# Attention feeding a routed two-layer network: two batches share six rounds of sums and gate products

## The chip, the cores and the metric

The kernel runs on one core of one Trainium2 chip. The metric is the device time of one execution in microseconds (us). TensorE (PE) multiplies matrices into PSUM, ScalarE (ACT) and VectorE (DVE) read PSUM and work elementwise, GpSimd (POOL) works on SBUF alone, and SyncE (SP) issues most transfers.

## What is computed

Attention over q, k and v of shape (8 batches, 12 heads, 448 positions, 64), then a routed network over the 3584 tokens that it gives:

```
scores = cap * tanh(q k^T / sqrt(64) / cap)
attn   = exp(scores - max) / (sum of them + 1e-9)
x      = (attn v), heads side by side        # 3584 x 768
logits = x @ w_gate                          # 8 experts
assign each token to one expert, best logits first, 448 tokens an expert
out[tokens of e] = relu(x[tokens of e] @ w1[e]) @ w2[e]
```

## The kernel before, in words

`attention` (L18) works through 24 groups of four heads, three groups to a batch: group g belongs to batch b = g//3 and is the batch's m = g%3, so m=0, 1 or 2. The order of the instructions on PE, ACT, DVE and SP is the order in which the loop at L330 writes them; no scheduler moves them. A batch is called odd or even by b.

In one pass of the loop, group g's scores are made and group g-1's values are summed:

- `qk(g,r)`, r=0 to 6: four matmuls of 64x64 tiles that run beside each other write a score tile to PSUM (`psS`, **two** buffers). I call this a score step, and number the steps of a group 1 to 7. ScalarE's tanh (L201) reads the tile and so frees its buffer. After steps 2 and 4 ScalarE does the exp of the two tiles (L206, 128x1792), after step 7 that of three (128x2688). From g=18 on (`G2`, and in the first groups) the first two exps are put off until after one more tanh.
- `avq(g-1,..)`: seven value steps of the same size into two PSUM tiles `psA` (two buffers, both in use); `av_out` on DVE copies them to `xT` at the end of the pass and so frees them for the next pass.
- On DVE: `av_out` of the pass before, `tr` (32x32 transposes of the next group's k, later of its q, into `tk` and `tq`), `esum` (the additions that form the row sums: 'e2' and 'r' for group g-1, 'e1' for group g).

Beside this each batch has work of its own, done while the next batch's groups run:

- **Rounds** (`rnd`, L262): a PSUM tile `psM` (pool `pM`, two buffers) has four strips of 32 rows. Sums of exps (`ones` against `es`) and products with `w_gate` (`gw` against `xT`) are accumulated in it. A round is up to four matmuls of 128x32 tiles, one per strip, that run beside each other. Four rounds make a batch:

```
R=[gate(0)+sums(0),gate(1)+sums(1),sums(2),gate(2)]
```

  Rounds 0 and 1 use all strips, the sums those at the ends (0 and 3) and the gates the middle ones (1 and 2). In rounds 2 and 3 only strips 0 and 3 have work. `pos` says which place each pair of heads has in the strips.
- `logit_in` and `logit`: DVE copies the tile, PE transposes it, DVE takes reciprocals of the sums, multiplies and adds up to logits `L1`.
- `xt(b,p)`, p=0 to 5, for batches 0 to 3: PE transposes `xT`, DVE multiplies with the reciprocals into `xn`, and SP writes `xn` to DRAM after p=5. The other batches' turn comes after the attention.
- `on_logits` (18 small DVE instructions that prepare a batch's routing keys, from L519 on) and `on_turn` (one transposed block of keys).

Where they stand before: in m=0 the turns of p=0 to 3 of batch b-2 and `on_logits(b-2)`; in m=1 the turns of p=4 and 5, and rounds 0 and 1 of batch b-1; in m=2 rounds 2 and 3, and the logits of b-1. For b=6 and 7 the rounds are one stage earlier and spread over all three groups. The routing search (`Routing`) and the experts (`ffn_all`) follow the attention.

Of the kernel before, what the change touches and what calls it, by code (L numbers as in the profile page):

```python
# [17 lines left out]
def attention(nc, tc, c1, xp, ep, nv, pM, q, k, v, cap, w_gate, xs, L1, ident, on_logits, on_turn, NDEF, xd, setup, mark):  # L18
# [3 lines left out]
    B,H,S,D=q.shape  # L22
    CP=112; NJ=S//CP; NP=H//2; NQ=NP//2; E=w_gate.shape[1]; HG=2
    N=B*NQ
    pos=lambda p: (1+p//2+2*(p%2)) if p<4 else 5*(p-4)
    whole=lambda g: 0<g<N-1
    xT={}; rin={}; xn={}; spilled={}; todo=list(range(B-NDEF,B-2))
    def xt(b,p,late=None):
        if late and todo:
            for n in todo:  # L30
                xT[n]=late[1].tile([128,NP,S],F32,name="xTr",bufs=len(todo))
                nc.sync.dma_start(xT[n],spilled[n])
            todo.clear()
        if p==0:
            alt=late and (b in spilled and (b-B)%2 or b==B-1)
            xn[b]=(late[1] if alt else xp).tile([CP,NJ,H,D],F32,name="xn",bufs=1)
        ps=late[0].tile([128,512],F32,name="psL") if late else pM.tile([128,512],F32,name="psM")
        for j in range(NJ):
            nc.tensor.transpose(ps[:CP,j*128:(j+1)*128],xT[b][:,p,j*CP:(j+1)*CP],ident)  # L39
        def rest():  # L40
            if b==B-1 and p==NP-1:
                for j in range(NJ):
                    for h in range(2):
                        q=4*(p//2)+p%2+2*h; o=2*pos(p)+h
                        nc.scalar.activation(xn[b][:,j,q,:],ps[:CP,j*128+h*D:j*128+h*D+D],AF.Copy,scale=rin[b][:,j,o:o+1])
# [8 lines left out]
            (nc.gpsimd if late else nc.vector).tensor_tensor(xn[b][:,:,h0:h0+3:2,:],src,  # L54
                rin[b][:,:,2*pos(p):2*pos(p)+2].unsqueeze(3).broadcast_to([CP,NJ,2,D]),op=ALU.mult)
            if p==NP-1 or (late and p==3) or (b==B-1 and p==1):
                c0=0 if not late or p==1 or (p==3 and b<B-1) else 4*D if p==3 else 8*D; c1=2*(p+1)*D
                nc.sync.dma_start(xs[b*S:(b+1)*S,c0:c1].rearrange("(j p) d -> p j d",j=NJ),xn[b].rearrange("p j h d -> p j (h d)")[:,:,c0:c1])
        if late: return rest
        rest()  # L60
    with ExitStack() as ctx:
# [212 lines left out]
        def spill(bb):
            if B-NDEF<=bb<B-2:
# [2 lines left out]
        def logit_in(b):  # L278
            lgs[b]=xp.tile([128,S],F32,name="lg",bufs=1)
            nc.vector.tensor_copy(lgs[b],misc.pop(b)[:,:S])  # L280
        def logit(b,part=None,some=False,pool=None):
# [5 lines left out]
            if b not in rin: rin[b]=xp.tile([CP,NJ,H],F32,name="rin",bufs=max(NDEF,2))  # L287
            r=rin[b]
            if part is not None:
                va=ps[:CP,:].rearrange("p (a k) -> p a k",k=32)  # L290
                r2=xp.tile([CP,NJ*4],F32,name="rg1",bufs=1)
                nc.vector.reciprocal(r2,va[:,:,0])
                t=part
                nc.vector.tensor_tensor(t[:,:,0:4,:],va[:,:,16:24].rearrange("p (j g) e -> p j g e",g=4),
                    r2.rearrange("p (j g) -> p j g",g=4).unsqueeze(3).broadcast_to([CP,NJ,4,E]),op=ALU.mult)
            else:
                a,c=(1,5) if some else (0,6); n=2*(c-a)
                v3=ps[:CP,:].rearrange("p (j k) -> p j k",k=128)
                sm=ps[:CP,:].rearrange("p (j s k) -> p j s k",s=8,k=16)[:,:,0::7,a:c]
                rr=r.rearrange("p j (a h) -> p j h a",h=2)[:,:,:,a:c]  # L300
                nc.vector.reciprocal(rr,sm)
                t=xp.tile([CP,NJ,n,E],F32,name=f"lt{n}",bufs=1)
                nc.vector.tensor_tensor(t,v3[:,:,16+16*a:16+16*c].rearrange("p j (s e) -> p j s e",e=E),
                    r[:,:,2*a:2*c].unsqueeze(3).broadcast_to([CP,NJ,n,E]),op=ALU.mult)
            if not some:
                nc.vector.tensor_reduce(L1[:,b*NJ:(b+1)*NJ,:],t.rearrange("p j s e -> p j e s"),axis=AX.X,op=ALU.add)
                if b>=B-2: on_logits(b)
                if b==B-1: on_turn(b)
                if part is not None: nc.vector.tensor_copy(r.rearrange("p j (a k) -> p j a k",k=2)[:,:,0::5,:],r2.rearrange("p (j a k) -> p j a k",j=NJ,k=2))  # L309
                return  # L310
            t1=xp.tile([CP,NJ,5,E],F32,name="lt1",bufs=1)
            nc.vector.tensor_reduce(t1[:,:,4,:],t.rearrange("p j s e -> p j e s"),axis=AX.X,op=ALU.add)
# [16 lines left out]
        part=None  # L329
        for g in range(N):  # L330
# [7 lines left out]
            if g==N-5: vgate()  # L338
            if g==N-3: vback()
            qk(g,0); qk(g,1)  # L340
            early=bb-1<B-NDEF; late=not early
            if early and bb>0 and m<2:
                for p in ((0,1),(4,5))[m]: xt(bb-1,p)
            if m==2 and bb>=0:
                if early:
                    for r in (2,3): rnd(bb,r)
# [4 lines left out]
            if m==2 and bb>=0 and early:  # L351
                logit_in(bb); spill(bb)
            for w in ('e2','r'): esum(g-1,w)
            if g==N-6: vturn()
            if not head: qk(g,2)
            if order: avq(g-1,2,0)
            if m==2 and late: rnd(bb,3)
            qk(g,3)
            if order: qk(g,4)
            if m==0:  # L360
                if early and bb>0: xt(bb-1,2); xt(bb-1,3)
                if not early: rnd(bb,0); rnd(bb,1)
                if bb>0: on_logits(bb-1)
            if m==1 and bb>=0:
                if early: rnd(bb,0); rnd(bb,1)
                else:
                    rnd(bb,2); spill(bb)
                if bb>0: on_turn(bb-1)
            if m==2 and late: logit_in(bb)
            if m==2 and bb>=0 and (early or b==B-1): logit(bb)  # L370
            tr(g+1,1)
            if order: qk(g,5)
            else: qk(g,4)
            avq(g-1,0,1)
            if head: qk(g,6)
            avq(g-1,1,1)
            if not order: qk(g,5); avq(g-1,2,1)
            if not head: qk(g,6)
            if order: avq(g-1,2,1)
            avq(g-1,3,1)  # L380
            if not last: esum(g,'e1')
            if g: av_out(g-1,0); av_out(g-1,1)
            if m==2 and late and b<B-1: logit(bb)
        g=N-1; b=B-1
        rnd(b,0,1); rnd(b,1,1)
        logit_in(b)
# [795 lines left out]
```

## Time and profile before

| | us |
|---|---|
| runs | 861.40, 861.65, 862.03; median 861.65 |
| profiled execution, its own time | 861.69 |
| its span, first to last instruction | 859.9 |
| busy in the span: PE, ACT, DVE, POOL | 835.1, 582.3, 617.8, 390.5 |

The attention takes about the first 325 us of the span; the granted TensorE clock is 1.0 in all slices. From then on routing and experts follow, which the change does not touch. A chain row of the profile gives start, length, and what ran, merged where the same line repeats; a score or value step shows as 8 matmul records (x8), a full round as 8, a transposition as 1.

### The profile page before, as it was taken

The numbers are of one execution on the slowest core, as the hardware profiler recorded it, in microseconds if no ns is written. First come the engines' busy times: TensorE is split into PE (matmuls) and PEld (weight loads), VectorE is DVE, ScalarE is ACT, GpSimd is POOL, SyncE is SP. The second block draws the span as 40 slices with busy tenths as digits, with TensorE's granted clock in tenths as the row PEclk, the third lists the DMA queues.
The fourth block names the chain that finished last, engine by engine and source line by source line (L and its number), as shares of the span: only waits on it lengthen the run. The fifth ranks groups of instructions, "written<-read, shape, count | busy, mean of one in ns | idle before, by whom it ended". The sixth has DMA issues, their size and how long they took to land.

```text
span 859.9 us, 16866 instructions
## 1 busy us (share of the span) xinstructions
PE 835.1 (97%) x5838; PEld 589.2 (69%) x5838; DVE 617.8 (72%) x1992; ACT 582.3 (68%) x776; POOL 390.5 (45%) x556
## 2 busy tenths in 40 slices
PE   6999999999999998899999999999999999999997
PEld 3334444444433334588888888888898889999997
DVE  5787988989897967876877987968878864263210
ACT  6998898989899887575284584575655754544421
POOL 8210000000000007675377497595677668859851
PEclk9999999999999999999999999999999999999999
DMA  8979877585986007870863896986978959959921
GB/s 145 163 122 166 180 130 151 108 173 93 218 189 125 2 2 253 253 239 0 281 204 107 238 278 208 284 250 226 262 213 238 298 161 239 309 191 295 287 74 56
DMA packets 368485, 159.28 MB, mean 185 GB/s; under 512 B 287088, under 2 KB 355312, under 8 KB 367888
## 3 DMA queue, kind: packets, MB, share of 16 engines
q1 hardware_dynamic: 357728, 128.30, 60.9%
q0 software_dynamic: 4688, 22.02, 7.6%
q10 hardware_dynamic: 5984, 7.88, 2.6%
q8 instruction: 46, 0.75, 0.4%
q14 instruction: 39, 0.32, 0.1%
HBM read 107.24 MB, written 42.66 MB: 174 GB/s over the span
## 4 chain that ended last, share of the span: by engine, by line
PE 72%; issue 7%; ACT 7%; DVE 5%; DMA 3%; SPq 3%; POOL 2%; ACTq 0%; POOLq 0%; DVEq 0%
PE psH L995 22%; PE psH L1057 18%; PE psA L240 12%; PE psS L200 12%; ACT e L201 3%; PE psM L272 3%; ACT e L206 2%; DVE cmpD L587 1%; PE psM L39 1%; POOL out_dram L1015 1%; DMA xz<-xgl 1%; DMA xg<-xz 1%; SPq L1039 1%; SPq L861 1%; SPq L939 1%
## 5 line engine op out<-in xcount | busy, mean ns | idle before, releaser
L1057 PE MATMUL psH<-hh,w2h 128*128 128x448 f32 x672 | 185.3, 367 | 0.0
L201 ACT ACTIVATE e<-psS 128x896 f32<-128x896 f32 x168 | 147.5, 910 | 26.4 <-PE psS L200 20.8
L200 PE MATMUL psS<-tq,tk 64*64 64x448 f32 x1248 | 141.1, 542 | 8.3 <-ACT e L201 7.7
L206 ACT ACTIVATE e<-e,bias 128x1792 f32<-128x1792 f32 (+2 forms) x74 | 147.3, 1992 | 1.8
L995 PE MATMUL psH<-xgh,w1h 128*128 128x448 f32 (+1 forms) x384 | 141.8, 369 | 0.1
L995 PE MATMUL psH<-xgh,w1l 128*128 128x448 f32 (+1 forms) x384 | 140.0, 365 | 0.0
L995 PE MATMUL psH<-xgl,w1h 128*128 128x448 f32 (+1 forms) x384 | 135.4, 366 | 0.0
L873 POOL TENSOR_TENSOR w2l<-w2r,w2h 128x768 fp32r<-128x768 f32 x64 | 131.1, 2052 | 9.2 <-ACT w2h L866 8.4
L873 POOL TENSOR_TENSOR w1l<-w1r,w1h 128x768 fp32r<-128x768 f32 x62 | 114.9, 1854 | 43.2 <-ACT w1h L866 43.2
L240 PE MATMUL psA<-e,nv 64*64 64x448 f32 x1232 | 134.1, 538 | 0.0
L1057 PEld LDWEIGHTS psH<-hh,w2h 128*128 128x128 f32 x672 | 124.8, 188 | 7.7
L535 POOL TENSOR_SCALAR r_Bt<-r_b 112x4 f16<-112x4 int32 x1 | 0.2, 199 | 272.4 <-DVE rin L309 272.4
L1057 PE MATMUL psH<-hh,w2l 128*128 128x448 f32 x336 | 115.2, 366 | 0.0
L200 PEld LDWEIGHTS psS<-tq,tk 64*64 64x64 f32 x1248 | 46.9, 132 | 79.2 <-issue 45.8
L240 PEld LDWEIGHTS psA<-e,nv 64*64 64x64 f32 x1232 | 49.4, 133 | 66.0 <-issue 61.9
L995 PEld LDWEIGHTS psH<-xgh,w1h 128*128 128x128 f32 x384 | 72.5, 189 | 4.8 <-ACT xgh L956 0.3
L995 PEld LDWEIGHTS psH<-xgl,w1h 128*128 128x128 f32 x384 | 72.3, 188 | 4.4 <-DVE xgl L957 0.2
L866 ACT ACTIVATE w2h<-w2r 128x768 fp32r<-128x768 f32 x64 | 75.0, 1184 | 0.5 <-DMA w2r<-in_moe_w_dram 0.5
L995 PEld LDWEIGHTS psH<-xgh,w1l 128*128 128x128 f32 x384 | 72.2, 188 | 4.4
L1004 ACT ACTIVATE hh<-psH 128x448 fp32r<-128x448 f32 x56 | 30.4, 543 | 60.4 <-PE psH L995 57.0
L1057 PEld LDWEIGHTS psH<-hh,w2l 128*128 128x128 f32 x336 | 63.2, 188 | 4.0
L898 POOL DMA_INDIRECT xg<-xs,idx x32 | 32.5, 1014 | 65.3 <-DVE zz L750 37.6
(397 smaller groups left out, 1392.8 us busy)
## 6 DMA issues: line engine op xcount, KB each, us to landing
w1r<-in_moe_w_dram SPq DMA_DIRECT2D x64, 384.0 KB, 7.1
w2r<-in_moe_w_dram SPq DMA_DIRECT2D x64, 384.0 KB, 6.4
k<-in_k_dram SPq DMA_DIRECT2D x92, 112.0 KB, 3.0
q<-in_q_dram SPq DMA_DIRECT2D x92, 112.0 KB, 3.0
nv<-in_v_dram SPq DMA_DIRECT2D x88, 112.0 KB, 3.3
yb<-yq SPq DMA_DIRECT2D x56, 168.0 KB, 5.1
on<-yb SPq DMA_DIRECT2D x7, 1152.0 KB, 7.6
xs<-xn SPq DMA_DIRECT2D x4, 1344.0 KB, 6.3
```

Of the source, the lines that this page charges most:

```text
L39: nc.tensor.transpose(ps[:CP,j*128:(j+1)*128],xT[b][:,p,j*CP:(j+1)*CP],ident)
L200: nc.tensor.matmul(ps[w:w+64,h,:S],tks[g,0][hp,o,r*64:r*64+64],tks[g,1][hp,o,:],start=True,stop=True)
L201: nc.scalar.activation(ev(g,r),ps[:,:,:S],AF.Tanh,scale=sr[0])
L206: act=lambda: nc.scalar.activation(e,e,AF.Exp,scale=sr[1],bias=bias)
L240: for h in range(2): nc.tensor.matmul(avp[g,o][h*64:h*64+64,:S],z[w,r,h,:],ev(g,r)[w,h,:],start=r==0,stop=r==6)
L272: nc.tensor.matmul(ps[k*32:k*32+32,:S],lhs,rhs,start=r==0 and i==0,stop=r==last or (r==1 and k in (1,2)))
L866: nc.scalar.activation(view(h),r,AF.Copy)
L873: (eng or nc.gpsimd).tensor_tensor(view(l),r,view(h).bitcast(F32),op=ALU.subtract)
L898: g=nc.gpsimd.indirect_dma_start(out=row(j,n),out_offset=None,in_=xs,in_offset=bass.IndirectOffsetOnAxis(ap=res[p][0][:n,j:j+1],axis=0))
L995: nc.tensor.matmul(ps[:,o:C],a[:,c,:],b[:,c,o:],start=(m==0 and o==0),stop=(m==DC*3-1)); m+=1
L1004: nc.scalar.activation(h,ps[:,:C],AF.Relu)
L1057: nc.tensor.matmul(ps[:,:C],spl[p,2,hf,f//2][w][:,f%2,cc*128:cc*128+128],h[:,a,f],start=(m==0),stop=(m==nm-1))
```

## The change

Batches 0 to 5 are taken in pairs (0,1), (2,3), (4,5). For the odd batch of a pair the strips are mirrored (`pos(p,1)`, `oneb`): its sums stand in the middle strips and its gates at the ends. So the half-empty rounds of the even batch are filled with sums of the odd one: four rounds in `both`, two in `rest`, six for two batches where there were eight. Batches 6 and 7 keep `rnd`. Around it, everything is placed anew:

- in m=2 of an odd batch b: `both(b-1)` between score steps 4 and 5; no rounds in m=1 of an odd batch nor in m=2 of an even one;
- in m=1 of an even batch: `rest(b-1)` ahead of the value steps;
- logits of both batches of a pair: in m=0 and m=2 of the next even batch, split in two on DVE;
- turns: for an odd b as before, but on DVE those of p=2,3 behind the q transposes; for an even b the turns of p=0 to 3 go through two **score buffers** (`pairs`, one buffer for two turns), those of p=4,5 behind step 4 of m=1;
- `on_logits` in m=1 and m=2 of odd batches; `on_turn(3)` and `on_logits(4)` in b=6.

```diff
+    other=lambda b: b<B-2 and b%2==1
+    pos=lambda p,b=0: (0,4,1,5,2,3)[p] if other(b) else pos0(p)
...
+        def both(a):
+            b=a+1
+            for m in range(2):
+                for o in range(2): put(a,1+o,'g',m,o,m==0,m==1)
+                for h in range(2): put(a,3*h,'s',m,h,m==0,False)
+            for h in range(2):
+                put(a,3*h,'s',2,h,False,False); put(b,1+h,'s',0,h,True,False)
+            for h in range(2):
+                put(a,3*h,'g',2,h,False,True); put(b,1+h,'s',1,h,False,False)
+        def rest(b):
+            for o in range(2):
+                put(b,3*o,'g',1,o,True,False); put(b,1+o,'g',2,o,False,False)
+            for o in range(2):
+                put(b,3*o,'g',0,o,False,True); put(b,1+o,'s',2,o,False,True)
...
+            if new:
+                if not odd and m==0: turn.append(lambda: logit(b-2,lazy=True))
+                if not odd and m==2 and b<B-2: turn.append(lambda: logit(b-1,lazy=True))
...
+            two=xn_ and not odd and m==0
+            def pairs(p):
+                ps=pS.tile([128,2,512],F32,name="psS")
+                for i in range(2): xt(b-2,p+i,ps=ps[:,i])
+            if new and not odd and m==1: rest(b-1)
...
+            esum(g-1,'e2')
+            if two: pairs(0)
+            esum(g-1,'r')
...
+            if new and odd and m==2: both(b-1)
             tr(g+1,1)
+            if new:
+                if odd and m==0 and b>1: xt(b-2,2); xt(b-2,3)
+                if not odd and m==1 and xn_: xt(b-2,4); xt(b-2,5)
+                if odd and m==2: logit_in(b-1); spill(b-1)
+                if b==B-2 and m==1: spill(b-1); on_turn(3); on_logits(4)
+                if odd and m==1 and b>1: on_logits(b-3)
+                if odd and m==2 and b>1: on_logits(b-2)
+            if two:
+                qk(g,4); avq(g-1,1,1); pairs(2); qk(g,5); avq(g-1,2,1); qk(g,6)
```

In the logits of an odd batch the multiplication is three instructions of 112x128 in place of one of 112x384. POOL makes `oneb` with 13 more memsets in the first microseconds.

How PE's order moves in m=0 of an even batch (here b=2; psS is a score buffer, psA the value tiles). Before:

```order
L200 MATMUL psS<-tq,tk 64x448 x8
L39 MATMUL psM<-ident,xT 112x128 x8
L240 MATMUL psA<-e_942,nv 64x448 x8
L240 MATMUL psA<-e_982,nv 64x448 x4
L200 MATMUL psS<-tq,tk 64x448 x8
L39 MATMUL psM<-ident,xT 112x128 x8
L200 MATMUL psS<-tq,tk 64x448 x4
L240 MATMUL psA<-e_982,nv 64x448 x4
```

And in the change:

```order
L314 MATMUL psM<-ident,lg 112x128 x4
L247 MATMUL psA<-e_945,nv 64x448 x8
L247 MATMUL psA<-e_979,nv 64x448 x4
L41 MATMUL psS<-ident,xT 112x128 x8
L207 MATMUL psS<-tq,tk 64x448 x4
L247 MATMUL psA<-e_979,nv 64x448 x4
L207 MATMUL psS<-tq,tk 64x448 x8
L247 MATMUL psA<-e_1017,nv 64x448 x4
L41 MATMUL psS<-ident,xT 112x128 x8
L207 MATMUL psS<-tq,tk 64x448 x4
```

The logits' transposes come first, each turn of two pairs takes a score buffer, and score steps 3, 4, 5 and 6 have moved against the value steps.

PE's order in m=2 of an odd batch in the change (here b=3), from score steps 3 and 4 to step 5:

```order
L207 MATMUL psS<-tq,tk 64x448 x8
L286 MATMUL psM<-xT,gw 32x448 x2
L286 MATMUL psM<-es,ones 32x448 x2
L286 MATMUL psM<-xT,gw 32x448 x2
L286 MATMUL psM<-es,ones 32x448 x3
L286 MATMUL psM<-es,oneb 32x448
L286 MATMUL psM<-es,ones 32x448
L286 MATMUL psM<-es,oneb 32x448
L286 MATMUL psM<-xT,gw 32x448
L286 MATMUL psM<-es,oneb 32x448
L286 MATMUL psM<-xT,gw 32x448
L286 MATMUL psM<-es,oneb 32x448
```

Sixteen matmuls, four rounds, stand together where four transposes of logits stood; the two rounds ahead of the value steps are gone.

DVE's order at the end of m=1 of an odd batch in the change (here b=3; the r_K rows are the last two of `on_logits`, et the 'e1' sum, xT<-psA `av_out`):

```order
L592 TENSOR_TENSOR r_VC<-r_P,r_Ct 112x32
L593 TENSOR_TENSOR r_K_373<-r_At,r_Bt 112x4
L601 SCALAR_TENSOR_TENSOR r_K_374<-r_kk,r_Ct 112x4
L218 TENSOR_TENSOR et<-e_1586,e_1633 128x1792
L268 COPY xT<-psA 128x448 x2
L187 STREAM_TRANSPOSE tk<-k 128x896
```

Before, these 18 instructions stood in m=0 ahead of the q transposes; now they stand behind those, ahead of 'e1' and `av_out`, in m=1 and again in m=2.

## Rows read from the trace of the kernel before

**Rows 1.** Busy time by stretch, batch 3's three groups: us, PE, PEld, DVE, ACT, POOL, PEclk, DMA, GB/s

```profile
133.33:173.31 39.98, 39.85 (x389) 17.16 (x389) 35.59 (x53) 36.17 (x31) 0.00 (x0) 1.00 0.70 139
```

**Rows 2.** Chain that ended last: start us, us, what; group 4, then groups 10 to 12

```profile
59.44 2.39 PE psM L272 x20
...
133.33 1.74 PE psS L200 x16
135.06 1.01 PE psM L39 x8
136.08 2.60 PE psA L240 x24
...
140.19 1.64 PE psM L272 x16
...
147.25 1.50 PE psS L200 x16
148.75 1.63 PE psM L272 x8
150.38 2.42 PE psA L240 x24
...
154.30 0.58 PE psM L286 x4
...
160.30 1.50 PE psS L200 x16
```

**Rows 3.** ScalarE in order of time: start, us, what; group 4, group 11, groups 18 to 20

```profile
59.40 1.71 ACT L201 ACTIVATE e<-psS 128x896 f32<-128x896 f32 x2
...
147.51 2.54 ACT L206 ACTIVATE e<-e,bias 128x2688 f32<-128x2688 f32 x1
149.96 1.70 ACT L201 ACTIVATE e<-psS 128x896 f32<-128x896 f32 x2
...
155.39 1.79 ACT L206 ACTIVATE e<-e,bias 128x1792 f32<-128x1792 f32 x1
157.09 1.94 ACT L201 ACTIVATE e<-psS 128x896 f32<-128x896 f32 x2
...
240.67 2.54 ACT L206 ACTIVATE e<-e,bias 128x2688 f32<-128x2688 f32 x1
...
253.12 2.54 ACT L206 ACTIVATE e<-e,bias 128x2688 f32<-128x2688 f32 x1
...
258.18 0.92 ACT L201 ACTIVATE e<-psS 128x896 f32<-128x896 f32 x1 [0.91 <-PE psS L200]
...
265.88 2.54 ACT L206 ACTIVATE e<-e,bias 128x2688 f32<-128x2688 f32 x1
...
278.09 2.54 ACT L206 ACTIVATE e<-e,bias 128x2688 f32<-128x2688 f32 x1
```

**Rows 4.** VectorE in order of time, group 9 (m=0 of batch 3) and group 10's begin

```profile
120.38 1.16 DVE L261 COPY xT<-psA 128x448 f32<-128x448 f32 x2 [0.33 <-PE psA L240]
...
123.65 1.10 DVE L180 STREAM_TRANSPOSE tk<-k 128x896 f32<-128x896 f32 x1
...
128.83 1.28 DVE L54 TENSOR_TENSOR xn<-psM,rin 112x512 f32<-112x512 f32 x2
130.03 0.18 DVE L519 TENSOR_REDUCE r_m<-L 112x4 f32<-112x32 f32 x1
...
132.08 1.10 DVE L180 STREAM_TRANSPOSE tq<-q 128x896 f32<-128x896 f32 x1
133.10 1.98 DVE L211 TENSOR_TENSOR et<-e,e 128x1792 f32<-128x1792 f32 x1
135.01 1.15 DVE L261 COPY xT<-psA 128x448 f32<-128x448 f32 x2
```

**Rows 5.** Groups by shape, VectorE: line, what, count, busy us, mean ns, idle before

```profile
L303 DVE TENSOR_TENSOR lt<-psM,rin 112x384 f32<-112x384 f32 x6 | 3.3, 558 | 0.2
```

**Rows 6.** The page's busy tenths of POOL in 40 slices of 21.5 us

```profile
POOL 8210000000000007675377497595677668859851
```

More of the change, by code (lines that the diff above doesn't have):

```diff
@@ L24, in attention, with xt @@
     N=B*NQ
-    pos=lambda p: (1+p//2+2*(p%2)) if p<4 else 5*(p-4)
+    pos0=lambda p: (1+p//2+2*(p%2)) if p<4 else 5*(p-4)
+    other=lambda b: b<B-2 and b%2==1
+    pos=lambda p,b=0: (0,4,1,5,2,3)[p] if other(b) else pos0(p)
     whole=lambda g: 0<g<N-1
     xT={}; rin={}; xn={}; spilled={}; todo=list(range(B-NDEF,B-2))
-    def xt(b,p,late=None):
+    def xt(b,p,late=None,ps=None):
         if late and todo:
@@ L36, in xt @@
             xn[b]=(late[1] if alt else xp).tile([CP,NJ,H,D],F32,name="xn",bufs=1)
-        ps=late[0].tile([128,512],F32,name="psL") if late else pM.tile([128,512],F32,name="psM")
+        if ps is None: ps=late[0].tile([128,512],F32,name="psL") if late else pM.tile([128,512],F32,name="psM")
         for j in range(NJ):
@@ L54, in rest @@
             (nc.gpsimd if late else nc.vector).tensor_tensor(xn[b][:,:,h0:h0+3:2,:],src,
-                rin[b][:,:,2*pos(p):2*pos(p)+2].unsqueeze(3).broadcast_to([CP,NJ,2,D]),op=ALU.mult)
+                rin[b][:,:,2*pos(p,b):2*pos(p,b)+2].unsqueeze(3).broadcast_to([CP,NJ,2,D]),op=ALU.mult)
             if p==NP-1 or (late and p==3) or (b==B-1 and p==1):
@@ L111, in attention @@
                 for h in range(HG): nc.gpsimd.memset(ones[64-64*o:128-64*o,m,h,16*h+pos(2*m+o):16*h+pos(2*m+o)+1],1.0)
+        oneb=c2.tile([128,NQ,HG,32],F32,name="oneb")
+        nc.gpsimd.memset(oneb,0.0)
+        for m in range(NQ):
+            for o in range(2):
+                for h in range(HG): nc.gpsimd.memset(oneb[64-64*o:128-64*o,m,h,16*h+pos(2*m+o,1):16*h+pos(2*m+o,1)+1],1.0)
         one0=c2.tile([128,2,HG,32],F32,name="one0")
@@ L272, in rnd, with put @@
                     nc.tensor.matmul(ps[k*32:k*32+32,:S],lhs,rhs,start=r==0 and i==0,stop=r==last or (r==1 and k in (1,2)))
+        def put(b,k,kind,m,n,start,stop):
+            if b not in misc: misc[b]=pM.tile([128,512],F32,name="psM")
+            for i in range(2 if b==0 and m==0 and kind=='s' else 1):
+                if kind=='g': lhs=gw[:,2*m+n,:]; rhs=xT[b][:,2*m+n,:]
+                elif b==0 and m==0: lhs=one0[:,i,n,:]; rhs=es_t[0][:,i,n,:]
+                else: lhs=(oneb if other(b) else ones)[:,m,n,:]; rhs=es_t[b*NQ+m][:,n,:]
+                nc.tensor.matmul(misc[b][k*32:k*32+32,:S],lhs,rhs,start=start and i==0,stop=stop)
+        def both(a):
[10 more added lines that the diff above has]
+                put(b,3*o,'g',1,o,True,False); put(b,1+o,'g',2,o,False,False)
+            for o in range(2):
+                put(b,3*o,'g',0,o,False,True); put(b,1+o,'s',2,o,False,True)
         lgs={}
@@ L280, in logit_in, with logit @@
             nc.vector.tensor_copy(lgs[b],misc.pop(b)[:,:S])
-        def logit(b,part=None,some=False,pool=None):
+        def logit(b,part=None,some=False,pool=None,lazy=False):
             if b not in lgs: logit_in(b)
@@ L286, in logit @@
                 mark[0]=nc.tensor.transpose(ps[:CP,j*128:(j+1)*128],lg[:,j*CP:(j+1)*CP],ident)
[L287 to L312, printed above, removed]
+            def scale():
+                if b not in rin: rin[b]=xp.tile([CP,NJ,H],F32,name="rin",bufs=max(NDEF,2))
+                r=rin[b]
+                if part is not None:
+                    va=ps[:CP,:].rearrange("p (a k) -> p a k",k=32)
+                    r2=xp.tile([CP,NJ*4],F32,name="rg1",bufs=1)
+                    nc.vector.reciprocal(r2,va[:,:,0])
+                    t=part
+                    nc.vector.tensor_tensor(t[:,:,0:4,:],va[:,:,16:24].rearrange("p (j g) e -> p j g e",g=4),
+                        r2.rearrange("p (j g) -> p j g",g=4).unsqueeze(3).broadcast_to([CP,NJ,4,E]),op=ALU.mult)
+                else:
+                    a,c=(1,5) if some else (0,6); n=2*(c-a)
+                    v3=ps[:CP,:].rearrange("p (j k) -> p j k",k=128)
+                    sm=ps[:CP,:].rearrange("p (j s k) -> p j s k",s=8,k=16)[:,:,2::3,a:c] if other(b) else ps[:CP,:].rearrange("p (j s k) -> p j s k",s=8,k=16)[:,:,0::7,a:c]
+                    rr=r.rearrange("p j (a h) -> p j h a",h=2)[:,:,:,a:c]
+                    nc.vector.reciprocal(rr,sm)
+                    yield
+                    t=xp.tile([CP,NJ,n,E],F32,name=f"lt{n}",bufs=1)
+                    if other(b):
+                        for u in range(3):
+                            nc.vector.tensor_tensor(t[:,:,4*u:4*u+4],v3[:,:,48*u:48*u+32].rearrange("p j (s e) -> p j s e",e=E),
+                                r[:,:,4*u:4*u+4].unsqueeze(3).broadcast_to([CP,NJ,4,E]),op=ALU.mult)
+                    else: nc.vector.tensor_tensor(t,v3[:,:,16+16*a:16+16*c].rearrange("p j (s e) -> p j s e",e=E),
+                        r[:,:,2*a:2*c].unsqueeze(3).broadcast_to([CP,NJ,n,E]),op=ALU.mult)
+                if not some:
+                    nc.vector.tensor_reduce(L1[:,b*NJ:(b+1)*NJ,:],t.rearrange("p j s e -> p j e s"),axis=AX.X,op=ALU.add)
+                    if b>=B-2: on_logits(b)
+                    if b==B-1: on_turn(b)
+                    if part is not None: nc.vector.tensor_copy(r.rearrange("p j (a k) -> p j a k",k=2)[:,:,0::5,:],r2.rearrange("p (j a k) -> p j a k",j=NJ,k=2))
+                    return
+                t1=xp.tile([CP,NJ,5,E],F32,name="lt1",bufs=1)
+                nc.vector.tensor_reduce(t1[:,:,4,:],t.rearrange("p j s e -> p j e s"),axis=AX.X,op=ALU.add)
+                yield t1
@@ L313, in logit @@
+            z=scale()
+            if lazy: return lambda: next(z,None)
+            t1=None
+            for t1 in z: pass
             return t1
@@ L340, in attention @@
             qk(g,0); qk(g,1)
[L341 to L346, printed above, removed]
-            order=g>=G2 or 0<g<4; head=0<g<4
+            new=0<b<B-1; odd=b%2==1; xn_=new and b<B-2
+            turn=[]
+            if new:
+                if not odd and m==0: turn.append(lambda: logit(b-2,lazy=True))
+                if not odd and m==2 and b<B-2: turn.append(lambda: logit(b-1,lazy=True))
+                if xn_ and b>1:
+                    if odd and m<2:
+                        for p in ((0,1),(4,5))[m]: xt(b-2,p)
+            order=g>=G2 or 0<g<4; head=0<g<4
+            lg=[z() for z in turn]
+            two=xn_ and not odd and m==0
[3 more added lines that the diff above has]
+            if new and not odd and m==1: rest(b-1)
             for j in range(1 if head else 2 if order else 3): avq(g-1,j,0)
@@ L350, in attention @@
             tr(g+1,0)
-            if m==2 and bb>=0 and early:
-                logit_in(bb); spill(bb)
-            for w in ('e2','r'): esum(g-1,w)
+            if new and not odd and m==1: logit_in(b-1)
+            if lg: lg[0]()
+            esum(g-1,'e2')
+            if two: pairs(0)
+            esum(g-1,'r')
             if g==N-6: vturn()
+            for z in lg: z()
             if not head: qk(g,2)
             if order: avq(g-1,2,0)
-            if m==2 and late: rnd(bb,3)
+            if two: avq(g-1,0,1)
@@ L358, in attention @@
+            if m==2 and b==B-1: rnd(bb,3)
             qk(g,3)
             if order: qk(g,4)
[L360 to L370, printed above, removed]
@@ L371, in attention @@
-            tr(g+1,1)
-            if order: qk(g,5)
-            else: qk(g,4)
[L374 to L379, printed above, removed]
+            if b==B-1 and m==0: rnd(bb,0); rnd(bb,1); on_logits(bb-1)
+            if b==B-1 and m==1: rnd(bb,2); spill(bb)
+            if m==2 and b==B-1: logit_in(bb); logit(bb)
+            if new and odd and m==2: both(b-1)
@@ new lines, in attention @@
+            tr(g+1,1)
+            if new:
[7 more added lines that the diff above has]
+                qk(g,4); avq(g-1,1,1); pairs(2); qk(g,5); avq(g-1,2,1); qk(g,6)
+            elif order: qk(g,5)
+            else: qk(g,4)
@@ L380, in attention @@
+            if not two:
+                avq(g-1,0,1)
+                if head: qk(g,6)
+                avq(g-1,1,1)
+                if not order: qk(g,5); avq(g-1,2,1)
+                if not head: qk(g,6)
+                if order: avq(g-1,2,1)
             avq(g-1,3,1)
@@ L382, in attention @@
             if g: av_out(g-1,0); av_out(g-1,1)
-            if m==2 and late and b<B-1: logit(bb)
+            if m==2 and b==B-2: logit(bb)
         g=N-1; b=B-1
```

## The prediction

> **What bounds the kernel now.** First the busy time of one batch's three groups [rows 1]: of 39.98 us PE is busy 39.85, ScalarE 36.17, VectorE 35.59. PE bounds, but the other two are within a tenth of it, so what PE gives up is only worth what they let through. Then the chain of waits [rows 2]: in batch 3 it is PE alone, and it gives the length of each group, from one pair of score steps to the next: m=1 takes 147.25-133.33 = 13.92, m=2 13.05, and m=0 the rest of 39.98, 13.01. It also gives prices: sixteen records of score steps take 1.50, so a step is 0.75 and the fourteen steps of a group 10.5; two rounds take 1.64, two turns 1.01, a batch's logit transposes 0.58. What follows such a piece is 0.16 or so longer (2.42 for three value steps in place of 2.25). A place with two rounds is thus worth 1.80, one with logits 0.74, one with two turns 1.17.
>
> Next ScalarE's order of time [rows 3]. A group begins there 0.26 behind PE's (147.51 against 147.25) with the long exp; the first tanh follows 2.45 later, two tanh take 1.70, an exp 1.70 until the next tanh can start. Last VectorE's [rows 4]: in m=0 the q transposes end at 133.18, and PE's next group starts at 133.33; that chain also passes 0.13 through this wait.
>
> **Part 1, rounds.** Per pair of batches eight rounds become six: 2 x 0.75 on PE, and two of four places go, 2 x 0.3: 2.1. Moving the q transposes ahead of the multiplications and `on_logits` in m=0 frees PE of waits of 0.13, 0.24 (the 1.74 score pair) and 0.18 (2.60 against 2.42), once a batch. PE's own work in a pair falls by 3.2. But a saving counts only in the group it falls in, since PE can lead ScalarE by two score buffers. So I go group by group.
>
> **How short a group can be.** With nothing but score and value steps, ScalarE runs: long exp at 0.26, tanh at 2.71, exp at 4.41, third tanh at 6.11, done at 6.97 (0.86 is half of 1.71 [rows 3]). Score step 5 needs that buffer: it starts at 7.0, and with the six steps behind it the group ends at 7.0 + 7 x 0.75 = 12.3. Here row and rule can be weighed. PE's count alone would end the two lightened groups at 11.7 and 11.2. The Trainium skill (TensorEngine Tiling (Array Packing), Performance Considerations, PSUM Bottleneck) says that tiling speeds up TensorE but not the reading of PSUM, which may become the bottleneck. By that rule the group is ScalarE's and ends at 12.3, by PE's count alone a pair would be 1.7 shorter; I go by ScalarE's rows.
>
> **The six groups of a pair** (before: 13.01, 13.92, 13.05, twice; sum 79.96):
>
> - Odd, m=0: the same PE work without the wait of 0.13: 12.88.
> - Odd, m=1: the rounds (1.80) and the two waits go; PE would need 11.7, ScalarE 12.3. **12.3.**
> - Odd, m=2: rounds (1.80) and logits (0.74) go, `both` comes, 4 x 0.75 + 0.14 + 0.16 = 3.30: 13.81. But `on_logits` now stands in m=1 ahead of 'e1' and `av_out`. By [rows 4], with the multiplications at 128.83 moved out of the way, the q transposes of such a group start 8.5 in (128.83-120.33), `on_logits` at 9.5 (1.02 later), takes 2.05, 'e1' 1.91, and `av_out` runs from 13.5 to 14.6. The group is over at 12.3, so the copies end 2.3 into m=2, and the value steps, which want to begin at 1.5, wait 0.8. **14.6.** `both` itself finds its sums done (VectorE's last addition is some 7.7 in, the fourth round starts at 9.4).
> - Even, m=0: 10.5 + 0.74 + 2 x 1.17 = 13.6 on PE. But the turns take score buffers. Counting on: score pair 1.50, logits 2.08, three value steps 4.50, turns 5.51, step 3 6.42, value step 7.17, steps 4 and 5 to 8.67, value step 9.42, turns 10.43. Step 6 needs step 5's buffer, whose tanh waits for the exp of steps 3 and 4: tanh of step 4 until 8.83, exp until 10.53, tanh until 11.39. PE starts step 6 at 11.44 instead of 10.6 and needs four more steps: **14.4.**
> - Even, m=1: 10.5 + 1.80 (`rest`) + 1.17: 13.5.
> - Even, m=2: logits alone, 11.2 on PE, ScalarE 12.3: 12.3.
>
> Sum 80.0: the pair (2,3) with batches 3 and 4 gains **nothing**.
>
> **The other batches.** In batch 1, m=1 loses 2.39 of rounds (at 59.44) [rows 2]; step 5 waits for the third tanh, done at 60.3 [rows 3], and comes 1.7 earlier in all; m=2 has no `on_logits` ahead, hence 13.81, and 0.75 for batch 0's double first round (2.39 against 1.64): 14.56, +1.5. Batch 2 is as above, 40.2 against 40.0. Together 0.0. Batch 5 is like batch 3: 39.8 against 40.0, -0.2. Batch 6 has its exps put off by one tanh. There `rest` stands ahead of the value steps and so of step 3, for whose tanh ScalarE already waits 0.91 [rows 3]: +1.79. The groups' lengths by the long exps are 12.45, 12.76 and 12.21; ScalarE alone would need 12.76-0.91 = 11.85, so m=0 and m=2, which lose rounds, can give back 0.60 and 0.36 at most. I take +0.8; the ends are 0 (the wait is made up elsewhere) and +1.8 (nothing given back).
>
> Edits that cost nothing: the three-part multiplication (two more starts beside one of 0.56 [rows 5], three times), behind VectorE's 12.3 groups; the 13 memsets, on a POOL that idles for slices from 65 us on [rows 6]; SP's order is the same. Batch 7, search and experts are unchanged and start when the attention ends, so the shift passes through whole.
>
> **Sum:** 0.0 + 0.0 - 0.2 + 0.8 = +0.6. The profiled execution took 861.69 (span 859.9 and 1.8 around it), 0.04 above the median: **862.3**, no change. About 0.2%, 1.7 us, is what a measurement of this kernel can tell from no change.
>
> **Rivals.**
>
> - *The two stalls don't come* (faster). The value steps' 0.8 in batches 3 and 5 and step 6's 0.85 in batches 2 and 4 rest on VectorE and ScalarE orders that I counted on by hand; if both fall away, 4 x 0.83 = 3.3 less: 859.0. For it: VectorE has 4.4 us a batch to spare [rows 1]. Against it: the queue order is fixed, and 'e1' stands ahead of `av_out`. Chance 0.27. If ScalarE also kept up in the light groups (1.7 a pair), 855; [rows 3] leave no room for it: 0.05.
> - *The score buffers held by VectorE* (slower). In m=0 of an even batch the second turns' multiplications must end before step 7 can start. I find VectorE done some 0.15 before; its list there (`av_out`, two transposes, three sums, four multiplications, the logits, 'e1') makes near 15 us against PE's 14.4. From 0.15 of lateness on, each us is a us for PE, and `av_out` then comes late for `rest` in the next group. With 1 us in each of the two groups and batch 6 at its end of +1.8: 862.3 + 2 + 1 = 865.3. The Trainium skill (Perfetto Trace Analysis, Optimization Strategy) says that the same gap repeating on the engine that should be saturated can mean that there is not enough PSUM for the next tile; by that rule PE would show a gap at each of these turns, as in this rival. Before, no such gap is in the chain [rows 2]. Chance 0.2.
> - *The shared rounds don't run side by side*, since two of them write two PSUM tiles: then two rounds a pair take double, 3 x 1.5 more: 866.8. Score steps also write two banks at once and run beside each other, which speaks against it: 0.04.
>
> **Chances.** Forecast 0.44, and the rivals as given. My own case reaches a little over +0.2%, so: faster by over 0.2% 0.31, within 0.43, slower 0.26. The range takes in most of the first two rivals: 858.4 to 865.2.
>
> **What would show it.** Right: groups of 12.3 in m=1 of odd and m=2 of even batches with ScalarE gapless up to its fifth tanh; a PE gap near 0.8 ahead of the value steps in m=2 of batches 3 and 5, released by `av_out`; one of about 0.85 ahead of step 6 in m=0 of batches 2 and 4, released by ScalarE; in batch 6's m=1 a ScalarE wait of over 2 us for step 3; rounds of 0.75 in `both`. Wrong: PE without gaps in the heavy groups, a batch pair of 78 us or less (first rival), or step 4 or 7 waiting for VectorE's multiplications (second).

## The result, and the profile after

The changed kernel takes 868.65 us (median of 6 runs, 868.02 to 869.0) against 861.52 for the kernel before beside it: a ratio of 1.0082, interval [1.0069, 1.0095]. It is 7 us slower, outside the range. The profiled execution took 868.55, its span is 866.7.

Busy time first, from the page of the changed kernel:

```profile
PE 831.1 (96%) x5838; PEld 585.1 (68%) x5838; DVE 620.2 (72%) x1998; ACT 582.0 (67%) x776; POOL 395.2 (46%) x569
```

PE does 4.0 us less than before (835.1) and the span is 6.8 longer: the saving was made, and PE waits for more than it saved. Where, the long exps of ScalarE tell, one per group; the same timeline has the light group 10 and batch 6:

```profile
135.99 2.54 ACT L213 ACTIVATE e<-e,bias 128x2688 f32<-128x2688 f32 x1
138.44 1.70 ACT L208 ACTIVATE e<-psS 128x896 f32<-128x896 f32 x2
140.17 1.80 ACT L213 ACTIVATE e<-e,bias 128x1792 f32<-128x1792 f32 x1
141.87 1.71 ACT L208 ACTIVATE e<-psS 128x896 f32<-128x896 f32 x2
...
148.58 2.54 ACT L213 ACTIVATE e<-e,bias 128x2688 f32<-128x2688 f32 x1
...
163.65 2.54 ACT L213 ACTIVATE e<-e,bias 128x2688 f32<-128x2688 f32 x1
...
246.03 2.54 ACT L213 ACTIVATE e<-e,bias 128x2688 f32<-128x2688 f32 x1
...
258.18 2.54 ACT L213 ACTIVATE e<-e,bias 128x2688 f32<-128x2688 f32 x1
...
265.06 0.92 ACT L208 ACTIVATE e<-psS 128x896 f32<-128x896 f32 x1 [2.73 <-PE psS L207]
...
272.76 2.54 ACT L213 ACTIVATE e<-e,bias 128x2688 f32<-128x2688 f32 x1
...
284.91 2.54 ACT L213 ACTIVATE e<-e,bias 128x2688 f32<-128x2688 f32 x1
```

From one long exp to the next, all groups of the pairs (us):

| group | forecast | measured | off, in all |
|---|---|---|---|
| odd, m=0 | 12.88 | 12.88, 12.88 | 0.0 |
| odd, m=1 (batches 1, 3, 5) | 12.3 | 12.59 three times | +0.9 |
| odd, m=2 (batches 1, 3, 5) | 14.56, 14.6, 14.6 | 14.78, 15.07, 14.64 | +0.7 |
| even, m=0 | 14.4 | **16.19, 16.19** | **+3.6** |
| even, m=1 | 13.5 | 13.50, 13.50 | 0.0 |
| even, m=2 | 12.3 | 12.58, 12.58 | +0.6 |
| batch 6 | 37.42+0.8 | 38.88 | +0.7 |

The misses sum to 6.4, and 862.3 + 6.4 = 868.7 is the time of the profiled execution but for 0.14. Batch 6 is 284.91-246.03 = 38.88, before it was 278.09-240.67 = 37.42 [rows 3].

The chain of waits shows step 5 of group 4, then m=2 of batch 3 (from 148.3) and m=0 of batch 4 (from 163.38):

```profile
60.30 0.98 PE psS L207 x8
61.29 1.50 PE psA L247 x16
...
149.63 0.63 DVE xT L268
150.26 0.04 issue
150.31 2.63 PE psA L247 x22
...
154.81 3.14 PE psM L286 x32
...
163.38 1.50 PE psS L207 x16
164.88 0.58 PE psM L314 x4
165.46 2.42 PE psA L247 x24
167.88 0.59 PE psS L41 x4
168.47 0.02 issue
168.50 0.70 DVE xn L56
169.20 0.04 issue
169.24 0.66 PE psS L41 x4
...
174.03 1.10 DVE tq L187
175.13 0.59 DVE xn L56
175.71 0.04 issue
175.76 0.65 PE psS L41 x4
176.41 0.91 PE psS L207 x8
...
179.57 1.50 PE psS L207 x16
```

Before, batch 3's chain was PE alone [rows 2]. Now VectorE stands in it: once for the copies `av_out` (149.63, the forecast stall), and in m=0 of the even batch at every pair of turns. The two turns of a pair are written to one buffer, and in the program's order the first's multiplication stands ahead of the second's transposes, so PE waits for VectorE between them (168.50, then 175.13), although the two fill different halves of the buffer (`ps[:,i]`). Busy time by engine (PE, PEld, DVE, ACT, POOL, each with its count, then PEclk, DMA share and GB/s) in that group and in light group 10:

```profile
163.38:179.57 16.19, 14.04 (x137) 6.00 (x132) 13.57 (x15) 12.20 (x11) 0.00 (x0) 1.00 0.38 61
135.73:148.32 12.59, 11.93 (x124) 4.92 (x120) 11.16 (x28) 11.91 (x11) 0.00 (x0) 1.00 0.71 179
```

In the long group no engine is busy for more than 14.04 of 16.19 us: it waits round a ring, not on one engine.

### The profile page after: what moved, and what is told of

Its sections match the earlier page's. It is cut to its first block, busy times and chain, and to the rows that moved or that the text cites. A ratio compares the mean times of both kernels' runs of the same rounds, so it can differ in the third digit from the quotient of the medians.

```text
span 866.7 us, 16881 instructions
## 1 busy us (share of the span) xinstructions
PE 831.1 (96%) x5838; PEld 585.1 (68%) x5838; DVE 620.2 (72%) x1998; ACT 582.0 (67%) x776; POOL 395.2 (46%) x569
## 4 chain that ended last, share of the span: by engine, by line
PE 71%; issue 9%; ACT 8%; DVE 8%; DMA 2%; POOL 2%; SPq 0%; ACTq 0%; POOLq 0%; DVEq 0%
PE psH L1049 23%; PE psH L1111 22%; PE psA L247 9%; PE psS L207 9%; ACT e L208 4%; ACT e L213 3%; PE psM L286 2%; DVE cmpD L641 1%; DVE et L218 1%; POOL out_dram L1069 1%; DVE es L218 1%; PE psM L41 1%; DVE tq L187 1%; DMA q<-in_q_dram 1%; PE psR L647 1%
## 5 line engine op out<-in xcount | busy, mean ns | idle before, releaser
L247 PEld LDWEIGHTS psA<-e,nv 64*64 64x64 f32 x1232 | 47.6, 133 | 68.4 <-issue 62.7
```

The source lines that it names most:

```text
L247: for h in range(2): nc.tensor.matmul(avp[g,o][h*64:h*64+64,:S],z[w,r,h,:],ev(g,r)[w,h,:],start=r==0,stop=r==6)
```

## The experiments

Three sets and a last run were made, each beside runs of the kernel before (medians 860.50, 860.79, 861.63 and 861.46). With the change's ratio of 1.0082 its own time there would be 867.6, 867.9, 868.7 and 868.5; these are worked out, not run. Where intervals overlap, the lengths of the groups in the traces decide: without an edit they repeat to 0.02 us from run to run, but for m=2 of batch 3 (14.90 to 15.07). The expectations call the keys that `on_logits` prepares "proposals".

### First set: the forecast's stalls one by one

**Both transposes of a pair ahead of both multiplications.**

```diff
-                for i in range(2): xt(b-2,p+i,ps=ps[:,i])
+                for z in [xt(b-2,p+i,ps=ps[:,i],hold=True) for i in range(2)]: z()
```

> The change with one edit: in m=0 of even batches both turns of a score buffer are transposed by PE before VectorE multiplies either. My theory (PE's second turn waits for VectorE's multiplication of the first, 0.78 and 1.37 us, because both write one tile): these waits go, the two groups shrink from 16.19 to 14.4 to 14.8, the time falls by about 3 us to 865.5. Rival (the score buffers are held by VectorE in any case, and the wait only moves to score steps 4 and 7): the groups stay at 16.2, the time at 868.6.

867.83 us, ratio 1.0084 [1.0067, 1.0101]: nothing gained. PE's timeline in m=0 of batch 4:

```profile
167.67 1.09 PE L41 MATMUL psS<-ident,xT 128*112 128x128 f32 x8
168.68 0.98 PE L207 MATMUL psS<-tq,tk 64*64 64x448 f32 x8
...
170.70 0.98 PE L207 MATMUL psS<-tq,tk 64*64 64x448 f32 x8 [0.29 <-ACT e L208]
172.72 0.98 PE L207 MATMUL psS<-tq,tk 64*64 64x448 f32 x8 [1.04 <-ACT e L208]
...
175.35 1.09 PE L41 MATMUL psS<-ident,xT 128*112 128x128 f32 x8 [0.89 <-ACT e L208]
```

The wait inside the pair is gone (x8 at 167.67, 1.01 to the next start as before), and yet the group is 16.88 (15.86 in batch 2). Steps 4 and 5 each wait until ScalarE has read the step ahead of them, as if one score buffer were left. By this my theory falls. But in this program as built, the addresses show that steps 3, 4 and 5 of this group and the second pair were given one and the same buffer (in batch 2 steps 3 and 4 one, steps 6 and 7 the other), while in the change, as before, the two buffers alternate. So the run changed two things; the last run below changes one.

**`on_logits` behind `av_out`.**

```diff
-                if odd and m==1 and b>1: on_logits(b-3)
-                if odd and m==2 and b>1: on_logits(b-2)
...
             if g: av_out(g-1,0); av_out(g-1,1)
+            if new and odd and m==1 and b>1: on_logits(b-3)
+            if new and odd and m==2 and b>1: on_logits(b-2)
```

> The change with on_logits in m=1 and m=2 of odd batches moved to the pass's end, behind 'e1' and av_out. Theory (av_out is late behind on_logits, so the value steps of m=2 in batches 3 and 5 wait): these groups shrink from 15.06 and 14.65 to about 13.9, the time by 1.5 to 2 us, to 866.9. Rival (VectorE is late anyway, the 2 us of keys then delay its first work of the next group and PE with it): within 0.5 us of the change, 868.6.

869.02 us, ratio 1.0096 [1.0079, 1.0113]: no gain. VectorE's timeline from m=2 of batch 3 into m=0 of batch 4, then PE's at the second turn there, and the busy time behind it (columns as above):

```profile
148.15 1.16 DVE L268 COPY xT<-psA 128x448 f32<-128x448 f32 x2 [0.91 <-PE psA L247]
...
151.32 1.11 DVE L187 STREAM_TRANSPOSE tk<-k 128x896 f32<-128x896 f32 x1
...
155.49 1.09 DVE L218 TENSOR_TENSOR es<-es,e 128x896 f32<-128x896 f32 x1
...
166.19 1.11 DVE L187 STREAM_TRANSPOSE tk<-k 128x896 f32<-128x896 f32 x1
...
170.17 1.10 PE L41 MATMUL psS<-ident,xT 128*112 128x128 f32 x4 [2.08 <-DVE xn L56]
...
170.10:173.50 3.40, 3.33 (x17) 1.49 (x21) 2.17 (x4) 0.46 (x1) 0.00 (x0) 0.51 0.32 50
```

The copies are early, but the keys' 2 us now stand ahead of everything else: the last sum, which the last round of `both` reads, ends at 156.6 and PE waits for it (m=2 is 14.93, within its spread; batch 5's grows from 14.64 to 14.88), and m=0 of batch 4, which has its logits and turns on VectorE, grows from 16.19 to 18.73. Not all of that is VectorE's. PE stood for 2.08 us at the second turn, and behind this wait the granted clock fell from 1.00 to 0.51, the lower of its two levels (1.2 instead of 2.4 GHz), for 3.4 us. PE's 3.33 us of work in them would take some 1.7 at the upper level (an estimate: half). The profiled execution was the longest of this run's four, 870.20; the others took 868.54 to 869.10.

**Batch 6's `rest` between score steps 4 and 5.**

```diff
-            if new and not odd and m==1: rest(b-1)
+            if new and not odd and m==1 and b<B-2: rest(b-1)
...
+            if b==B-2 and m==1: rest(b-1)
```

> The change with batch 6's rest (two rounds) behind score step 4 or 5 instead of ahead of the value steps; batches 2 and 4 as in the change. Theory (ahead of the value steps it delays step 3, for whose tanh ScalarE waits 2.73 us): batch 6 shrinks from 40.4 to about 39.0, the time by 1.0 to 1.5 us to 867.4. Rival (ScalarE's exps set batch 6 in any place of the rounds): 868.6.

865.92 us, ratio 1.0064 [1.0047, 1.0081]. Batch 6 is 12.15 + 13.22 + 12.15 = 37.52, that is 1.36 shorter and 0.10 from before. The theory holds: rounds ahead of score step 3 made ScalarE stand for 2.73 us (265.06 above). (`logit_in` of batch 5 moves behind the rounds with them.)

**A round more in each light group**, into a tile that nothing reads.

```diff
+            if (xn_ or b==1) and (odd and m==1 or not odd and m==2):
+                ds=pM.tile([128,512],F32,name="psM")
+                for kk in range(4): nc.tensor.matmul(ds[kk*32:kk*32+32,:S],gw[:,kk,:],xT[b-1][:,kk,:],start=True,stop=True)
```

> The change with one more round of four matmuls, into a tile that nobody reads, behind score step 4 in the light groups (m=1 of batches 1, 3, 5, m=2 of batches 2, 4): 5 x 1.05 us of PE work more. Theory (ScalarE sets these groups at 12.6 and PE waits in them): hidden but for 0.1 to 0.2 in m=1 of batches 3 and 5, so 868.6 to 869.2. Rival (PE sets them and what it is given it needs): 5 us more, 873.8.

868.13 us, ratio 1.0086 [1.0069, 1.0103]. Three of the five groups keep their 12.59, two have 12.75; behind the second of these batch 5's m=2 gives 0.15 back (batch 3's 14.91 lies in its spread). A round more costs 0 to 0.16 a group there: the light groups are ScalarE's.

### Second set: the buffers, the rounds, the keys

**The turns of m=0 one by one in the logits' buffer**, none in a score buffer.

```diff
-            def pairs(p):
-                ps=pS.tile([128,2,512],F32,name="psS")
-                for i in range(2): xt(b-2,p+i,ps=ps[:,i])
+            one=lambda p: xt(b-2,p,ps=lgt[0])
...
-                qk(g,4); avq(g-1,1,1); pairs(2); qk(g,5); avq(g-1,2,1); qk(g,6)
+                one(1); qk(g,4); avq(g-1,1,1); one(2); qk(g,5); avq(g-1,2,1); one(3); qk(g,6)
...
```

Score step 3, a value step and the second half of the logits on VectorE move ahead of the first turn with it.

> Change here: the four turns in m=0 of batches 2 and 4 are written one by one into the buffer of the logits just turned, none into a score buffer; PE has two more breaks between turns and score steps (0.16 each). Theory (a score buffer stays taken until VectorE has multiplied the turn out of it): m=0 of these batches falls from 16.2 to 14.4 us, which is VectorE's own list there (14.2 us of instructions), 3.6 us in two groups: 864.0 us. Rival (VectorE's list is late in any case, and PE waits for it wherever the turns stand): the groups stay over 15.5 us, 866.2 us or more.

867.36 us, ratio 1.0075 [1.0058, 1.0091]. The group is 15.65, the next one grew from 13.50 to 14.16: the rival's numbers. VectorE, then PE, in m=0 of batch 4:

```profile
172.91 1.10 DVE L187 STREAM_TRANSPOSE tq<-q 128x896 f32<-128x896 f32 x1
173.94 0.65 DVE L56 TENSOR_TENSOR xn<-psM,rin 112x512 f32<-112x512 f32 x1
...
174.65 0.65 PE L41 MATMUL psM<-ident,xT 128*112 128x128 f32 x4 [1.35 <-DVE xn L56]
```

The third turn waits for the second's multiplication, which stands behind two sums and the q transposes. So the rival could be true, or only this order bad; the third set tells these apart.

**The first round of `both` in m=1 of the odd batch.**

```diff
-            if new and odd and m==2: both(b-1)
+            if new and odd and m==1: both(b-1,(0,))
+            if new and odd and m==2: both(b-1,(1,))
```

> Change here: the first of the four rounds done for two batches moves from m=2 of odd batches to m=1, the light group. Theory (m=1 of odd batches is ScalarE's, PE has room for a round there): m=1 grows by 0.1 us, m=2 loses 0.75; three odd batches, 2.0 us less: 865.6 us. Rival (m=2 of odd batches waits for VectorE, which has the proposals in both groups): no gain, 867.6 us.

865.56 us, ratio 1.0055 [1.0038, 1.0071]: as the theory has it. In batches 3 and 5 m=1 is 12.75 (+0.16) and m=2 14.15 and 13.72 (-0.92 each); in batch 1 they are 13.26 (+0.67) and 13.53 (-1.25).

**Keys of the even batches in m=1 of an even batch.**

```diff
-                if odd and m==1 and b>1: on_logits(b-3)
+                if xn_ and not odd and m==1: on_logits(b-2)
```

> Change here: the proposals that stood in m=1 of batches 3 and 5 move to m=1 of the even batches ahead of them. Theory (they make the copies of the value sums late, and the value steps of m=2 wait for these): m=2 of batches 3 and 5 loses its wait of 0.5 us, m=1 of the even batches has 2 us of VectorE to spare: 866.5 us. Rival (what m=2 loses is made up at its rounds, as when the proposals were put last): 867.6 us.

865.58 us, ratio 1.0056 [1.0039, 1.0072]. m=2 of batches 3 and 5 is 14.02 and 14.01, m=1 of the even batches stays at 13.50: the theory holds. The keys ahead of `av_out` had cost 1.05 in batch 3 (0.9 by the low end of its spread) and 0.63 in batch 5.

**All of these together.**

> All of these at once, and the rest of the rounds of batch 5 put behind score step 4 in batch 6 (measured alone: 1.7 us). Theory (the four losses lie in different groups, so their gains add): 867.6 - 3.6 - 2.0 - 1.1 - 1.7 = 859.2 us, which is the kernel before at 860.5 or a little faster. Rival (ScalarE or VectorE takes over as the bound wherever PE is freed): half of that, 863.5 us.

863.74 us, ratio 1.0035 [1.0022, 1.0047]: the rival's number, but not shown to come by its reason. Of the 4.5 us that the theory is off, 3.6 are what it counted for the turns, which gave nothing (the first run of this set); and the round and the keys gain in one group, m=2 of odd batches, which falls to 13.54 where the two gains added would make 13.10. The pair (3,4) is 12.88 + 12.75 + 13.54 + 15.64 + 14.16 + 12.58 = 81.55 against 79.96 before; most of what is over it stands in m=0 of the even batch, 15.64 against 13.01.

### Third set: is it VectorE's order, or its load?

**Multiplications of turns ahead of VectorE's sums and transposes**, on top of the turns in the logits' buffer.

```diff
                 qk(g,2); avq(g-1,0,1); one(0)
-            esum(g-1,'r')
+            else: esum(g-1,'r')
...
+            if two: one(1); esum(g-1,'r'); qk(g,4); avq(g-1,1,1); one(2)
             tr(g+1,1)
...
-                one(1); qk(g,4); avq(g-1,1,1); one(2); qk(g,5); avq(g-1,2,1); one(3); qk(g,6)
+                qk(g,5); avq(g-1,2,1); one(3); qk(g,6)
```

> Change here: as in the run with the turns in the logits' buffer, but VectorE multiplies the first two turns ahead of the last two sums and the third ahead of the q transposes, so that no turn stands behind other work of VectorE's. Theory (what is left of the loss in m=0 of batches 2 and 4 is turns that wait for multiplications placed behind 2 to 3 us of VectorE's other work): the group falls from 15.64 to 14.2 us: 867.4 - 2.9 = 864.5 us. Rival (VectorE's 14.2 us of instructions with their gaps set the group): 15.3 us or more, 866.7 us.

865.56 us, ratio 1.0046 [1.003, 1.0063]; the group is 14.22 in both batches, as the theory has it. PE's timeline at the third turn of batch 4, the busy time of that group (columns as above), and `rest` behind it in the chain:

```profile
171.21 0.65 PE L41 MATMUL psM<-ident,xT 128*112 128x128 f32 x4
...
161.54:175.77 14.23, 14.23 (x137) 5.81 (x132) 12.60 (x15) 12.09 (x11) 0.00 (x0) 1.00 0.29 48
...
177.27 2.30 PE psM L286 x16
```

No turn waits any more: PE is busy for all of the group, VectorE for 12.60 of it. So its 14.22 are PE's own list, fourteen steps at 0.75, the logits and four single turns at 0.58 + 0.16 each, and not VectorE's load: the same VectorE work had stood in a group of 15.65. VectorE still ends late: the next group's `rest` needs the copies, takes 2.30 in place of 1.64, and that group stays at 14.17.

**Two of the four turns moved on to m=1**, on top of all edits.

```diff
-                one(1); qk(g,4); avq(g-1,1,1); one(2); qk(g,5); avq(g-1,2,1); one(3); qk(g,6)
+                qk(g,4); avq(g-1,1,1); one(1); qk(g,5); avq(g-1,2,1); qk(g,6)
...
-                if not odd and m==1 and xn_: xt(b-2,4); xt(b-2,5)
+                if not odd and m==1 and xn_: xt(b-2,2); xt(b-2,3)
...
                 avq(g-1,1,1)
+                if xn_ and not odd and m==1: xt(b-2,4); xt(b-2,5)
```

> Change here: the run with all edits, with two of the four turns of m=0 of batches 2 and 4 moved on to m=1, where VectorE has the room; m=0 keeps two, one by one in the logits' buffer. Theory (VectorE's load in m=0, 14.2 us, is what made the group long): m=0 has 12.9 us of VectorE and 12.5 of PE and falls from 15.64 to 12.9, m=1 grows from 14.16 to 14.7 with PE's second pair of turns (1.17, of which 0.66 was a wait for VectorE); two pairs, 4.4 us: 859.3 us, faster than before. Rival (with the proposals VectorE has 14.7 us in m=1, so the load only moves): m=1 at 15.5, 861 us.

860.19 us beside 861.63, ratio 0.9983 [0.9973, 0.9993]: 8.5 us under the change's worked-out time and 1.4 under the kernel before. The interval leaves out 1, but the difference is below the 0.2% that I had taken as the limit of what can be told. Windows of m=0 of batch 4, columns as above:

```profile
158.87:171.80 12.93, 12.93 (x132) 5.13 (x128) 11.98 (x13) 12.02 (x11) 0.00 (x0) 1.00 0.45 80
```

PE is busy for all of it. m=0 is 12.90 and m=1 14.68, as expected; the two together went from 29.69 in the change to 27.58. The reason in the theory, VectorE's load in m=0, is not what the runs show: with all four turns there and none waiting, m=0 was already PE's own 14.22. What moved is work of PE's: m=0 loses two single turns, and in m=1 the pair more (1.17) costs only 0.52, because `rest` no longer waits for the copies.

**The same with the keys left in odd batches.**

```diff
-                if xn_ and not odd and m==1: on_logits(b-2)
+                if odd and m==1 and b>1: on_logits(b-3)
```

> Change here: as the run with two turns moved, but the proposals stay in m=1 of the odd batches, where the change has them. Theory (VectorE's load decides): m=1 of the even batches loses 2 us of VectorE and is PE's, 14.7 us; m=2 of batches 3 and 5 gets its wait for the copies back, 0.6: 1.2 us more than with the proposals moved, or 860.5 us. Rival (the even m=1 was VectorE's with the proposals): 0.5 us or more below the run with the proposals moved.

860.75 us, ratio 0.9989 [0.9979, 0.9998]. m=1 of the even batches is 14.68 either way, so VectorE's list fits in it with the keys too; m=2 of batches 3 and 5 is 13.99 and 13.74 instead of 13.54. The theory's direction, at half its size (0.64 by these groups).

### The last run: the first one again, with the buffers in turn

```diff
-        pS=ctx.enter_context(tc.tile_pool(name="pS",bufs=2,space=PSUM))
+        pSS=[ctx.enter_context(tc.tile_pool(name="pS%d"%i,bufs=1,space=PSUM)) for i in range(2)]; nS=[0]
+        def stile():
+            nS[0]+=1
+            return pSS[nS[0]%2].tile([128,2,512],F32,name="psS")
```

> Change here: both transposes of a pair ahead of both multiplications, as in the first run, but the two score buffers are dealt strictly in turn; in that first run the build had given score steps 3, 4 and 5 of m=0 of batch 4 the same buffer. Theory (the first run showed its buffers, not the turns: with the buffers in turn the wait inside a pair is simply saved): the pair takes 1.01 us instead of 2.02, step 5 starts when ScalarE has read step 3, step 7 waits a little for the second pair's multiplication behind the q transposes, and m=0 of batches 2 and 4 is 14.4 to 15.0 us instead of 16.19: 2.4 to 3.6 us less than the change. Rival (a lent score buffer makes PE and ScalarE take turns wherever the multiplication stands): 15.8 us or more, no gain.

865.80 us, ratio 1.0051 [1.0035, 1.0068]; m=0 is 14.86 in both batches and m=1 stays at 13.50. The first score step of m=0 of batch 4 in the chain, then PE's timeline there:

```profile
162.04 1.50 PE psS L210 x16
...
166.47 1.09 PE L41 MATMUL psS<-ident,xT 128*112 128x128 f32 x8
167.48 0.98 PE L210 MATMUL psS<-tq,tk 64*64 64x448 f32 x8
...
169.03 1.72 PE L210 MATMUL psS<-tq,tk 64*64 64x448 f32 x16
...
171.44 1.09 PE L41 MATMUL psS<-ident,xT 128*112 128x128 f32 x8
173.66 0.98 PE L210 MATMUL psS<-tq,tk 64*64 64x448 f32 x8 [1.13 <-ACT e L211]
174.46 0.93 PE L250 MATMUL psA<-e,nv 64*64 64x448 f32 x8
175.21 0.93 PE L210 MATMUL psS<-tq,tk 64*64 64x448 f32 x8
```

Each pair is one piece, steps 4 and 5 stand together without a wait, and the one wait left is the forecast one: step 6, released by ScalarE. The theory holds, but for the small wait that it had at step 7 (175.21, none), and the rival is out: a lent score buffer is no harm in itself. By their addresses the buffers alternate here as in the change, so the order inside the pairs is all that differs from it. This order was not run together with the edits of the second set.

## Why the prediction was wrong

- **Even, m=0: the step that failed.** The term of 14.4 measured 16.19. "Turns 5.51, step 3 6.42" took a pair of turns at the 1.01 that it takes in two buffers of `psM` [rows 2]. Written as transposes, multiplication, transposes, multiplication into one buffer, the first pair takes 169.24+0.66-167.88 = 2.02, because PE waits for VectorE inside the pair; the second takes more, since its first multiplication stands behind the q transposes (174.03 in VectorE's order) and starts at 175.13. Step 6 came 176.41-163.38 = 13.03 into the group instead of 11.44. With the two transposes ahead of the two multiplications and the buffers in turn, step 6 comes 173.66-162.04 = 11.62 in, held by ScalarE as I had counted, and the group is 14.86 against 14.4. So 1.33 of the 1.79 was the order inside the pair; the rest is 0.18 at step 6, and a first step after a wait, which is dearer (below).
- **The second rival** had the right engine and the wrong place: VectorE held the buffer at the second transposes of a pair, not ahead of step 7, which waits for nothing in the change or in the last run. I had drawn the rival from VectorE's sum of work (near 15 us) and not from where each multiplication stands.
- **The rule on gaps.** PE does show a gap at both pairs of turns. The Trainium skill (Perfetto Trace Analysis, Optimization Strategy) reads such a repeating gap as a possible lack of PSUM for the next tile. The trace agrees on the place. More PSUM was not needed: the same two buffers with another order give 14.86, while leaving the score buffers alone, with turns that wait in the logits' buffer, still gave 15.65. Whether a further buffer would have closed the gap too was not run.
- **Light groups.** ScalarE has no gap from the long exp through the fourth tanh (135.99 to 143.6 above; the trace goes on without one through the sixth, to 147.05), and step 5 starts at 60.30, as forecast for group 4. What I missed is that the first step after PE has stood takes 0.98 in the chain and not 0.75 (60.30 above): 0.23 of the 0.28 in each of five groups.
- **Odd, m=2.** Right in kind: `both` takes 3.14, so its rounds of two tiles run beside each other and the third rival is out; the value steps wait for `av_out`. Without the keys in m=1 the groups are 14.02 (I had 13.81), and the keys cost 1.05 and 0.63 (I had 0.8).
- **Even, m=1 and odd, m=0.** Right to 0.01.
- **Batch 6.** Right in kind, the wait for step 3 is 2.73. I let m=0 and m=2 give back 0.96 of 1.79; they gave 0.36, both stopping at 12.15, so the cost was 1.46.
- The first rival (the stalls don't come) is refuted by the same groups.

## What to carry to other kernels

Where two writes share a buffer, write both before the first reader, and price a write by what stands ahead of its reader in that engine's queue, not by the write. Before work is moved into a stage, go through every engine's list there, and not only its sum: VectorE's work in m=0 of the even batch fitted into 14.22 us once no turn stood behind other work of it, and had made 15.65 in a worse order. Removing work from PE paid only where no wait for another engine took its place. And an edit may make the build deal the buffers anew: look at which buffer each tile got before reading a run as a verdict.

## What was not expected of the hardware

A score step that follows a wait of PE takes 0.98 us from its start to its end, and the next one starts 0.80 behind its start (173.66 to 174.46 in the last run). In an unbroken row a step takes 0.93, and the next starts after 0.75 (174.46 to 175.21): 0.18 of each step runs beside the begin of the next. A wait loses this overlap and 0.05 more, so each costs 0.23 beyond the idle time that the profile gives for it, at a granted clock of 1.0.
